# Attention outputs stored in two steps for pairs 1 to 14, and two projection steps per unit of attention at its end

## The chip, the cores and the metric

The kernel runs on one core of one Trainium2 chip. The metric is device time in microseconds (us) of one execution. All executions quoted here are fast: only those are compared. "Before" is the kernel before the change; it was run again in the same rounds as every other kernel, on the same chip.

## The reference, cut to what matters

The program has two independent parts; their outputs stand side by side. Part A is a state-space layer, which this text doesn't touch. Part B is attention over 64 segments of 32 tokens with 8 memory tokens each, 32 heads of 128, and an output projection:

```python
for s in range(n_seg):                       # 64 segments
    h = jnp.concatenate([mem, xs], axis=1)   # 8 memory rows, 32 new rows
    q, k, v = h @ Wq, h @ Wk, h @ Wv         # 32 heads of 128
    p = softmax(where(mask, q @ k.T * scale, -1e9))
    o = einsum('bhte,hed->btd', p @ v, Wo)   # output projection, 4096 -> 1024
    mem = o[:, :M, :]
    outs.append(o[:, M:, :])
```

The kernel guesses the memory rows, computes all segments at once, and checks the guess at the end. If it does not hold, a general path under a branch does the work again.

## The kernel before

The kernel issues in phases: part A's first stage with the values of part B, part A's second stage, attention, output projection. Attention goes by pairs of heads (`hp`, 16 pairs) and units (`u`, 11 a pair). The projections to queries and keys (`pr`) run ahead of it, so that TensorE (PE) has work while other engines compute exponentials. When they are used up, in the last units of the last pair, steps of the output projection (`first`) take their place. Cuts are marked with `...`.

```python
    def att_front(self, hp, u):              # scores, exponential, mask
        ...                                  # 4 matmuls on PE into s
        k.S.activation(e[:], s[0:GW, :, :, 0:GW], ACT.Exp, scale=float(E) ** -0.5, accum_out=...)
        m = self.mt[i % len(self.mt)]
        k.G.tensor_tensor(m[...], e[:], mask[...], ALU.mult)        # GpSimd (POOL)
        return [(hp, 4 * u + b, m, b) for b in range(4)]

    def att_back(self, blocks):              # values: 3 matmuls on PE from m, divided on VectorE
        ...
        early = hp == HP - 1

        def rows(g0, g1):
            r = on[64 + GX * (g0 - 1):64 + GX * (g1 - 1), :].rearrange("(g p) n -> p g n", p=GX)
            k.SP.dma_start(r[:, :, cs], ov[0:GX, g0:g1, :])
        if early and b0 + n == 2 * GE:       # half way: store what there is
            rows(1, GE)
            k.SP.dma_start(on[0:64, cs], ov[0:64, 0, :])
        if b0 + n == 2 * NG:                 # the pair is done
            if early:
                rows(GE, NG - 1)
            else:
                rows(1, NG - 1)
                k.SP.dma_start(on[0:64, cs], ov[0:64, 0, :])
            ...

    def attention(self):
        for hp in range(HP):
            for u in range(NU):
                ...
                pend += self.att_front(hp, u)
                back(8)                      # values lag two units (8 blocks) behind
                yield hp, u
        back(0)                              # the final flush
        yield HP, 0

    def outproj_first(self):                 # a step is four 128x512 matmuls
        ...
        for tt in range(3):
            ps.append(k.ps("P"))
            for h in range(0, 24, 4):        # 18 steps need heads 0 to 23 only
                self.out_mm(ps[tt], self.ol0, tt, 0, h, h + 4)
                yield
        ...                                  # from here on heads 24 to 31, b_ol

        for n, (hp, u) in enumerate(at):     # in kernel_main
            ...
            if done == 18 * HP:              # query/key projection used up
                if first is None:
                    ...
                    first = b.outproj_first()
                next(first)
        p3.close()
        ...
        f0 = nc.values_load(b.flag[0:1, 0:1], min_val=0, max_val=1)
        with tc.If(f0 == 1, preferred_fallthrough_block=True, label="general"):
            ...                              # the general path: not taken here
```

`SP` is the engine that issues most DMAs, in order. In attention a scheduler may reorder the matmuls of PE, so the program's text alone doesn't give the order; it was read from the built program.

## Time and profile before

| | before |
|---|---|
| time | 1247.49 us median of 3 runs (1247.3 to 1248.05) |
| PE busy | 1234.4 of 1245.6 us |
| waits of PE from 480 to 1030 us | 0.9 us, all on POOL's b_m |
| last copy of output to the end of the span | 4.4 us |

The first lines are from the page of before: the span; busy time of PE, its share and its instructions; and the chain of work that ended last, by engine.

```profile
span 1245.6 us, 20120 instructions
...
PE 1234.4 (99%) x8270; PEld 662.3 (53%) x8342; DVE 668.0 (54%) x1250; ACT 263.5 (21%) x631; POOL 275.8 (22%) x407
...
PE 98%; DMA 1%; issue 0%; ACT 0%; POOL 0%; DVE 0%; SPq 0%; ACTq 0%
```

This is the list of waits of PE in before, from 480 to 1030 us: who waited for whom, us in total, times, longest.

```profile
PE psO L64 <- POOL b_m L644: 0.9, 3, 0.4
```

The timeline of PE in before shows the three. Its columns are start, duration, engine, line, operation, output and inputs, shapes, number of matmuls merged, and in brackets the idle time before and what ended it. psS are scores, psO and psR values, psP with b_wv, b_vst or b_ol the output projection.

```profile
1008.39 0.34 PE L64 MATMUL psS<-b_q,b_k 128*128 128x99 bf16 x4
1008.57 0.28 PE L64 MATMUL psO<-b_v,b_m 128*128 128x129 bf16 x2
1009.05 0.23 PE L64 MATMUL psO<-b_v,b_m 128*128 128x129 bf16 x1 [0.20 <-POOL b_m L644]
1009.11 1.03 PE L64 MATMUL psP<-t,b_wv 128*128 128x512 bf16 x4
...
1011.53 0.22 PE L64 MATMUL psO<-b_v,b_m 128*128 128x129 bf16 x1
1012.01 0.29 PE L64 MATMUL psO<-b_v,b_m 128*128 128x129 bf16 x2 [0.26 <-POOL b_m L644]
1012.13 1.03 PE L64 MATMUL psP<-t,b_vst 128*128 128x512 bf16 x3
...
1015.42 0.39 PE L64 MATMUL psO<-b_v,b_m 128*128 128x129 bf16 x4
1016.24 0.29 PE L64 MATMUL psO<-b_v,b_m 128*128 128x129 bf16 x2 [0.43 <-POOL b_m L644]
1016.37 0.28 PE L64 MATMUL psR<-b_v,b_m 128*128 128x129 bf16 x2
...
1025.98 5.13 PE L64 MATMUL psP<-t,b_ol 128*128 128x512 bf16 x23
```

The SP queue of before, with the DMAs that the argument uses. The duration is the queue's own, not the transfer's.

```profile
936.50 0.40 SPq L64 DMA_DIRECT2D b_wq<-in_B_Wq_dram  x1
940.08 0.39 SPq L64 DMA_DIRECT2D b_wk<-in_B_Wk_dram  x1
...
1006.91 9.47 SPq L64 DMA_TRANSPOSE b_ol<-b_on  x1
...
1017.68 5.92 SPq L64 DMA_DIRECT2D b_on<-b_ob  x2
...
1024.84 17.64 SPq L64 DMA_TRANSPOSE b_ol<-b_on  x4
```

### The profile page before, as it was taken

To read this page: it belongs to the slowest core of one execution; us is meant where nothing else is said; L and a number is where in the kernel's file an instruction comes from. 1 tells how busy PE (TensorE), PEld (TensorE's weight loads), DVE (VectorE), ACT (ScalarE), POOL (GpSimd) and SP (SyncE) were. 2 spreads that over 40 slices of the span, in tenths; PEclk is the share of its full clock that TensorE was granted. 3 is DMA by queue.
4 is the path that set the end of the run, shared out by engine and by line. 5 is a ranking of instruction groups with operands and counts; after the bars stand their busy time and mean duration, and the time that the engine had idled before them with its cause. 6 is when DMAs were issued, how large, how long until landed. Compare 5 with 4: busy or idle time off the path is not lost.

```text
span 1245.6 us, 20120 instructions
## 1 busy us (share of the span) xinstructions
PE 1234.4 (99%) x8270; PEld 662.3 (53%) x8342; DVE 668.0 (54%) x1250; ACT 263.5 (21%) x631; POOL 275.8 (22%) x407
## 2 busy tenths in 40 slices
PE   9999999999999999999999999999999999999998
PEld 5444444444455555556666656555665554446444
DVE  4688899998711124666666666666666641001000
ACT  5344444443310000211112111111211110000000
POOL 4111331212332321322222222222222220000000
PEclk9999999999999999999999999999999999999999
DMA  9965444554898834664454544545473289407000
GB/s 245 272 192 148 131 132 128 144 156 107 241 323 247 251 116 95 192 167 123 95 144 108 144 108 114 138 92 133 96 155 95 61 223 220 110 18 153 17 17 27
DMA packets 316022, 176.83 MB, mean 142 GB/s; under 512 B 138650, under 2 KB 301326, under 8 KB 315926
## 3 DMA queue, kind: packets, MB, share of 16 engines
q1 hardware_dynamic: 293830, 147.95, 48.1%
q10 hardware_dynamic: 21072, 24.38, 5.9%
q0 software_dynamic: 1024, 3.17, 0.7%
q8 instruction: 66, 1.08, 0.4%
q14 instruction: 30, 0.25, 0.1%
HBM read 89.14 MB, written 53.17 MB: 114 GB/s over the span
## 4 chain that ended last, share of the span: by engine, by line
PE 98%; DMA 1%; issue 0%; ACT 0%; POOL 0%; DVE 0%; SPq 0%; ACTq 0%
PE psP L64 82%; PE psU L64 9%; PE psS L64 3%; PE psO L64 2%; PE psR L64 2%; DMA wo<-in_B_Wo_dram 1%; DMA b_xr<-in_B_x_dram 0%; ACT b_xe L89 0%; POOL b_m L644 0%; DVE b_ost L91 0%; SPq L64 0%; ACT b_e L641 0%; ACTq L89 0%
## 5 line engine op out<-in xcount | busy, mean ns | idle before, releaser
L64 PE MATMUL psP<-b_xe,b_wq 128*128 128x480 bf16 (+1 forms) x1280 | 247.7, 343 | 0.1
L64 PE MATMUL psP<-b_xe,b_wk 128*128 128x480 bf16 (+1 forms) x1280 | 247.7, 343 | 0.0
L64 PE MATMUL psP<-b_wv,b_xe 128*128 128x512 bf16 (+2 forms) x1033 | 223.4, 372 | 1.0 <-ACT b_xe L89 0.2
L644 POOL TENSOR_TENSOR b_m<-b_e,maskB 99x396 bf16<-99x396 bf16 x160 | 139.8, 874 | 334.0 <-ACT b_e L641 334.0
L641 ACT ACTIVATE b_e<-psS 99x396 bf16<-99x396 f32 x176 | 88.2, 501 | 532.2 <-PE psS L64 527.9
L64 PEld LDWEIGHTS <-b_wk 128*128 128x128 bf16 x1280 | 119.4, 98 | 94.2
L64 PEld LDWEIGHTS <-b_wq 128*128 128x128 bf16 x1280 | 118.7, 98 | 87.7
L64 PEld LDWEIGHTS <-b_xe 128*128 128x128 bf16 x1056 | 101.8, 98 | 119.1 <-ACT b_xe L89 0.4
L91 DVE CAST b_k<-psP 128x480 bf16<-128x480 f32 (+1 forms) x192 | 97.5, 529 | 101.1 <-PE psP L64 101.1
L91 DVE CAST b_q<-psP 128x480 bf16<-128x480 f32 (+1 forms) x192 | 97.5, 529 | 93.0 <-PE psP L64 91.4
L64 PEld LDWEIGHTS <-b_ol 128*128 128x128 bf16 x864 | 84.3, 98 | 94.4
L64 PE MATMUL psU<-a_xT,a_bt 128*128 128x512 bf16 x493 | 113.9, 379 | 1.1
L64 PE MATMUL psP<-t,a_hl 128*128 128x512 bf16 x496 | 112.1, 379 | 0.8
L91 DVE CAST b_ost<-psP 128x512 bf16<-128x512 f32 (+1 forms) x17 | 11.5, 676 | 183.4 <-PE psP L64 182.4
L64 PE MATMUL psP<-wo,b_ol 128*128 128x512 bf16 (+1 forms) x440 | 91.9, 364 | 0.4
L64 PE MATMUL psP<-t,b_ol 128*128 128x512 bf16 x408 | 91.7, 379 | 0.4
L280 POOL TENSOR_SCALAR a_tt<-a_pr,a_tabf 128x1 f32<-128x1 f32 x48 | 34.1, 709 | 243.5 <-DVE a_pr L275 243.5
L89 ACT ACTIVATE b_vst<-psP 128x512 bf16<-128x512 f32 x126 | 72.0, 589 | 71.0 <-PE psP L64 65.0
L661 DVE TENSOR_TENSOR b_ob<-psO,b_accR 99x384 bf16<-99x384 f32 x160 | 85.9, 553 | 2.0
L267 DVE TENSOR_TENSOR a_pr<-psU,a_tabf 128x2048 f32<-128x2048 f32 x32 | 73.0, 2282 | 15.7 <-PE psU L64 14.0
L64 PEld LDWEIGHTS <-a_bt 128*128 128x128 bf16 x512 | 49.2, 98 | 57.6
L64 PEld LDWEIGHTS <-a_hl 128*128 128x128 bf16 x512 | 49.1, 98 | 56.7
(200 smaller groups left out, 963.8 us busy)
## 6 DMA issues: line engine op xcount, KB each, us to landing
b_v<-b_vx SPq DMA_DIRECT2D x16, 1122.0 KB
b_wv<-in_B_Wv_dram SPq DMA_DIRECT2D x16, 1024.0 KB
b_on<-b_ob SPq DMA_DIRECT2D x15, 960.0 KB
b_vx<-b_vst ACTq DMA_DIRECT2D x24, 544.0 KB
a_hs<-a_h SPq DMA_DIRECT2D x32, 256.0 KB
b_wog<-in_B_Wo_dram SPq DMA_DIRECT2D x4, 2048.0 KB
b_wq<-in_B_Wq_dram SPq DMA_DIRECT2D x16, 512.0 KB
b_wk<-in_B_Wk_dram SPq DMA_DIRECT2D x16, 512.0 KB
```

Source lines behind the costliest of these rows:

```text
L64: r = f(*a, **kw)
L89: self.S.activation(out, in_, ACT.Copy)
L91: self.V.tensor_copy(out, in_)
L267: V.tensor_tensor(pr[:], u[:].unsqueeze(1).to_broadcast([128, 2, 2, TB]), view(t3, [[TB + 1, 2], [TB + 1, 2], [1, TB]]), ALU.mult)
L280: G.tensor_scalar(tt[:, j:j + 1], w[:, j, TB - 1:TB], t3[:, 1, TB:TB + 1], None, ALU.mult)
L641: k.S.activation(e[:], s[0:GW, :, :, 0:GW], ACT.Exp, scale=float(E) ** -0.5, accum_out=self.accE[0:GW, i:i + 1])
L644: k.G.tensor_tensor(m[0:GW, 0:4 * GP].rearrange("p (a b q) -> p a b q", a=2, b=2)[:, :, :, 0:GW], e[:], mask[0:GW, :, :].unsqueeze(2).to_b ...
L661: V.tensor_tensor(self.ob[:, b0:b0 + n, :], o[0:GW, 0:n, 0:E], r.unsqueeze(2).to_broadcast([GW, n, E]), ALU.mult)
```

## The change

It has two parts, numbered here as in the prediction. Part 1 takes two steps of the output projection instead of one with each of the last units of attention, to give PE something to do while it would wait for the mask. Part 2 stores each pair's outputs in two portions, as only the last pair's were stored before; its intent is presumably to spread the traffic. Pair 0 is left out.

```diff
@@ att_back
-        early = hp == HP - 1
+        early = hp > 0
@@ kernel_main
                     first = b.outproj_first()
                 next(first)
+                next(first)
         p3.close()
```

In the built program part 2 adds 14 DMA issues to SP. Part 1 leaves PE the same matmuls in another order from 1006 us on.

## The prediction

> **What bounds it.** TensorE. The page gives PE 1234.4 us busy of a 1245.6 us span (99%), and the chain of waits is 98% PE. By windows of time, PE is 430.0 of 430 us busy from 560 to 990 us. From 485 to 1030 us, all of attention and the start of the output projection, PE's list of waits has only three, on POOL's masked probabilities b_m, 0.9 us together. The timeline puts them in the last units of attention: 0.20 us before 1009.05, 0.26 before 1012.01, 0.43 before 1016.24.
>
> **Part 1, two projection steps per unit.** It only moves matmuls. In before, once the query/key projection is used up (1006 us), a unit of attention comes with one step: four 128x512 matmuls, 0.86 us (32 take 6.91 us in the timeline, 216 ns each; the Trainium skill, "TensorE: Matmul & The Clock Gate", section "Back-to-back issue gap", has N / 2.4 + 2.5 ns: the trace agrees). With scores and values a unit then costs PE about 1.3 us, while scores, exponential (0.50), accumulator read (0.19) and mask (0.87), with hand-overs, take about 1.9 us until values may start. So PE catches up with POOL three times. With two steps a unit costs 2.1 us. The compiled order of the changed kernel has eight such matmuls where four stood, in each of the last units and before the final flush, so each wait gets 0.86 us more cover. I expect all 0.9 us to vanish; PE is the chain, so all of it counts.
>
> What could give it back: attention ends about 5 us later (1016 to about 1022), so its last stores, issued at 1017.7, come at about 1023. The transposed loads of row block 1 follow in the SP queue (1024.8 to 1042.5, so to about 1048); first use is 1065.7, some 15 us of slack. The transposed load b_ol of the first row block depends on early stores only (issued 1006.9); PE reaches it after the same work, at about 1025. The steps taken inside attention use heads 0 to 23, loaded long before.
>
> **Part 2, stores in two steps for pairs 1 to 14.** 14 more DMA issues on SP (about 0.3 to 0.5 us each), same bytes. In the compiled order the early store now stands ahead of the next query and key weight loads and waits for DVE's b_ob. The Trainium skill, "DMA: Bandwidth & Descriptors", section "Anatomy of one DMA", says that the issuing sequencer waits, not the DMA engines; so the weight loads behind are delayed, an estimated 0 to 4 us. Their slack is about 37 us (issued 936.5, first used 973.5). No PE wait on a DMA shows in attention, so this wins and costs nothing.
>
> **Sum.** 1247.5 - 0.9 = 1246.6 us, 0.07%; range 1245.9 to 1247.9. Chances: faster 0.004, same 0.988, slower 0.008.
>
> **What would show it.** Right: no PE wait on b_m between 1005 and 1025; PE busy unchanged at 1234 us; attention's last matmul near 1022; b_ol's first matmul near 1025 without a wait; no PE idle in attention before 1005. Wrong: a PE or weight-load wait on a DMA (b_ol, wo, b_wq, b_wk, b_v), or a b_m wait left at the flush.
>
> **What would make it wrong.** The b_ol load lands just before its use, so reaching it 0.9 us sooner exposes it; or early stores, held in the SP queue, delay a pair's value or weight loads more than estimated. Either would cost 1 to 5 us.

## The result, and the profile after

The change took 1246.90 us median (1246.65 to 1247.20, 4 runs), and before 1247.47 (1247.30 to 1248.05; the three runs above and a fourth). The ratio is 0.9995, with a 95% interval of 0.9977 to 1.0012. Ratios here are the mean time of one kernel's fast runs over that of the other's of the same rounds, so not quite the ratio of the medians. Repeated in other rounds (last experiment) it was 0.13 us below before. So a difference exists at most in the tenths, and this document asks where the rest went, because the trace shows 1.4 us of PE time saved.

The page of the change:

```profile
span 1245.3 us, 20124 instructions
...
PE 1234.2 (99%) x8270; PEld 662.5 (53%) x8342; DVE 667.7 (54%) x1250; ACT 263.4 (21%) x631; POOL 275.8 (22%) x407
...
PE 99%; issue 0%; DVE 0%
```

The list of waits of PE from 480 to 1030 us is empty. The timeline of PE, at the same places:

```profile
1010.04 0.34 PE L64 MATMUL psS<-b_q,b_k 128*128 128x99 bf16 x4
1010.22 0.33 PE L64 MATMUL psO<-b_v,b_m 128*128 128x129 bf16 x3
1010.39 1.89 PE L64 MATMUL psP<-t,b_vst 128*128 128x512 bf16 x8
...
1020.58 0.50 PE L64 MATMUL psO<-b_v,b_m 128*128 128x129 bf16 x6
1020.92 0.28 PE L64 MATMUL psR<-b_v,b_m 128*128 128x129 bf16 x2
...
1024.49 5.13 PE L64 MATMUL psP<-t,b_ol 128*128 128x512 bf16 x23
```

The groups of three value matmuls take 0.17 us now (1010.22 to 1010.39), the six of the flush 0.34 (1020.58 to 1020.92) where before took 0.95 (1015.42 to 1016.37). The three savings are 0.37, 0.43 and 0.61 us, together 1.41. From the start of the last matmul on b_wk to that of the first on b_ol it is 20.03 us in before and 18.62 in the change: 1.42. From there to the last matmul both take 214.52 us.

The SP queue of the change:

```profile
937.79 1.31 SPq L64 DMA_DIRECT2D b_on<-b_ob  x2
939.21 0.53 SPq L64 DMA_DIRECT2D b_wq<-in_B_Wq_dram  x1
940.01 0.39 SPq L64 DMA_DIRECT2D b_wk<-in_B_Wk_dram  x1
...
1022.24 2.66 SPq L64 DMA_DIRECT2D b_on<-b_ob  x2
...
1026.41 17.62 SPq L64 DMA_TRANSPOSE b_ol<-b_on  x4
```

The query weights are issued 2.7 us later, behind the new early store, and nobody waits for them: the last matmul on b_wk starts at 1005.87 us, in before at 1005.95. Up to the end of the work the prediction holds, but for the size of what part 1 wins. Now the end. These are the last copy of the output on VectorE (DVE), and what SP waited for longest in its last lines: first before, then the change.

```profile
1240.81 0.42 DVE L91 CAST b_ost<-psP 128x256 bf16<-128x256 f32 x1 [6.24 <-PE psP L64]
...
SPq L1155 <- SPq L1155: 1.3, 2, 0.8
```

```profile
1239.32 0.42 DVE L91 CAST b_ost<-psP 128x256 bf16<-128x256 f32 x1 [6.24 <-PE psP L64]
...
SPq L1156 <- SPq L1156: 2.8, 1, 2.8
```

The work ends 1.49 us earlier, but the span only 0.35 us. The stretch from the end of that copy to the end of the span is 4.38 us in before and 5.51 in the change (unrounded records): 1.13 us were given back. And SP waits for itself, once, for 2.8 us. The records of SP's sequencer (the part of an engine that takes its instructions in order) around its last branch, with times from the end of the copy. DRAIN is the name of an instruction that stands a few times at its end:

```
                                     before    change
last output store issued              +0.03     +0.03
its data landed                       +1.21     +1.21
its semaphore complete                +1.70     +1.75
SP's last branch                      +0.41     +0.40
two instruction fetches, 8 KiB each   +1.51     +1.59
next instruction of SP                +0.95     +3.26
SP's first DRAIN                      +3.36     +4.61
end of the span                       +4.38     +5.51
```

The next instruction of SP checks a semaphore. In the change that semaphore belongs to a store issued at 1170.84 us, whose completion came at 1172.97. So SP did not wait for data. The records don't tell which engine the fetches are for. SP is the last engine to get to the common end: the other engines' last DRAIN before it starts at +0.90 at the latest, SP's at +3.55 in before and +4.69 in the change.

SP goes on 2.31 us later, and yet only 1.13 reach the end. In before SP goes on early, but its second check is for the last store: it passes at +1.72, when that store's semaphore is complete, 0.75 us after the first check; in the change, where the store is long done, the second check follows after 0.08. That is 0.67 us. And before loses about 0.44 us at the first DRAIN, which starts 0.36 us after the check in front of it and takes 0.13 (in the change 0.04 and 0.01).

### The profile page after: what moved, and what is told of

The parts are those of the page before. It is cut to its first block, busy times and chain, and to the rows that moved or that the text cites. A ratio compares the mean times of both kernels' runs of the same rounds, so it can differ in the third digit from the quotient of the medians.

```text
span 1245.3 us, 20124 instructions
## 1 busy us (share of the span) xinstructions
PE 1234.2 (99%) x8270; PEld 662.5 (53%) x8342; DVE 667.7 (54%) x1250; ACT 263.4 (21%) x631; POOL 275.8 (22%) x407
## 4 chain that ended last, share of the span: by engine, by line
PE 99%; issue 0%; DVE 0%
PE psP L64 82%; PE psU L64 9%; PE psS L64 3%; PE psO L64 2%; PE psR L64 2%; DVE b_xe L91 0%; DVE b_ost L91 0%; DVE a_n L962 0%; DVE hpb L105 0%; DVE ones L102 0%
```

## The experiments

The theory: part 2 of the prediction's count is wrong. The 14 added issues move the code of SP, which decides how long SP takes from its last branch to the end; part 1 alone is worth 1.4 us. Rivals: the end is longer because the work ends earlier, or by chance; the order of completions decides; or the split stores cost something themselves. For part 1 a rival says that the order of the projection matmuls, not the mask, is what counts.

In the table, "SP" is the number of SP's instructions in front of the final branches in the built program. "PE part" is the time from the start of the last b_wk matmul to that of the last matmul. "Stretch" runs from the end of the last copy to the end of the span. Time and difference are medians, in us; before is that of the same rounds.

| kernel | time | before | difference | SP | PE part | stretch |
|---|---|---|---|---|---|---|
| before | 1247.47 | | | 569 | 234.55 | 4.38 |
| change | 1246.90 | 1247.47 | -0.57 | 583 | 233.14 | 5.51 |
| e1_two_steps | 1246.04 | 1247.54 | -1.50 | 569 | 233.14 | 4.42 |
| e2_split_stores | 1248.56 | 1247.54 | +1.02 | 583 | 234.56 | 5.42 |
| e3_change_sp_hint | 1246.82 | 1247.54 | -0.72 | 584 | 233.13 | 5.41 |
| e4_two_steps_sp_hint | 1246.10 | 1247.54 | -1.44 | 570 | 233.13 | 4.39 |
| e5_before_pad16 | 1248.62 | 1247.32 | +1.30 | 586 | 234.56 | 5.39 |
| e6_before_pad8 | 1248.18 | 1247.32 | +0.86 | 578 | 234.56 | 5.52 |
| e7_change_moved14 | 1245.70 | 1247.32 | -1.62 | 569 | 233.13 | 4.34 |
| e8_zero_steps | 1247.03 | 1247.32 | -0.29 | 569 | 234.40 | 4.39 |
| e9_mask_on_vector | 1246.11 | 1247.07 | -0.96 | 569 | 233.26 | 4.35 |
| e10_three_steps | 1245.86 | 1247.07 | -1.21 | 568 | 233.13 | 4.46 |
| e11_two_steps_moved14 | 1245.09 | 1247.07 | -1.98 | 555 | 233.14 | 3.63 |
| e12_change_again | 1246.94 | 1247.07 | -0.13 | 583 | 233.13 | 5.49 |

All outputs were correct. All differences are within 0.2% of the time; the 95% intervals of the ratios contain 1 in every case but e11's (0.9970 to 0.9998). The case therefore rests on the two columns at the right more than on the timed differences. Each of their values is from one profiled execution; over all kernels of a kind they repeat within 0.01 us (PE part) and 0.13 us (stretch).

### Part 1 alone: e1_two_steps

```diff
+                next(first)
```

> Part 1 alone (two steps per unit, stores as in before). Both theories: no PE wait on b_m from 1005 to 1025 us, first b_ol matmul about 1.4 us earlier than in before (1025.98), last DVE copy of b_ost near 1239.3 us. Theory (the stretch from the end of that copy to the end of the span, 4.4 us in before and 5.6 in the change, grows because of the 14 added DMA issues on SP, which move SP's code): stretch 4.4 us, span near 1244.1, about 1.3 us faster than before, so about 1245.9 to 1246.2 on the clock. Rival (the stretch is longer because the work ends earlier, or varies by chance): stretch 5.0 to 5.6 us, no faster than the whole change (1246.9).

Measured: 1246.04 us (1245.75 to 1246.29) against 1247.54 (1247.17 to 1248.30): 1.50 us less, in ranges that don't meet. The PE part is that of the change, the stretch that of before. The last copy came at 1239.74, 0.4 us later than expected, because of another wait: PE waited 0.4 us at 492 us, labelled "issue", before the first value matmul of all. Such a wait of 0.2 to 0.4 us stands in the profiles of e3, e4 and e6 as well, and not in those of before or the change. It is not explained here; it is the reason that the stretches of a run are compared and not its absolute times. The rival that an earlier end makes a longer stretch falls: the work ends 1.1 us earlier than in before, and the stretch is 4.42.

### Part 2 alone: e2_split_stores

```diff
-        early = hp == HP - 1
+        early = hp > 0
```

> Part 2 alone (stores in two steps, one projection step per unit). Theory: PE as in before, three waits on b_m, 0.9 us as listed; last DVE copy near 1240.8 us; stretch after it 5.4 to 5.7 us instead of 4.4; 0.8 to 1.2 us slower than before, about 1248.4. Rival (stretch not tied to SP's issues): stretch 4.4 us, time as before, 1247.5.

Measured: 1.02 us slower (1247.95 to 1248.91, which overlaps before's 1247.17 to 1248.30), PE as in before with its three waits, stretch 5.42. The end of e2:

```profile
1240.73 0.42 DVE L91 CAST b_ost<-psP 128x256 bf16<-128x256 f32 x1 [6.24 <-PE psP L64]
...
SPq L1155 <- SPq L1155: 2.7, 1, 2.7
```

The copy ends when it does in before, and SP again has one wait for itself, 2.7 us. So the whole loss is part 2's, and behind the work. The two parts add up: -1.50 + 1.02 = -0.48, and the change measured -0.57.

### A branch hint for SP: e3_change_sp_hint and e4_two_steps_sp_hint

The kernel gives PE a hint about its final branch some 25 us ahead. If SP waits for the instructions at the branch's target, the same hint on SP might help.

```diff
-    k.tc.mark_branch_hint_location("general", "LikelyTaken", engines=[mybir.EngineType.PE])
+    for e in (mybir.EngineType.PE, mybir.EngineType.SP):
+        k.tc.mark_branch_hint_location("general", "LikelyTaken", engines=[e])
```

> The whole change, and in addition a branch prefetch hint on SP, beside the one that PE has, some 25 us before the branch at the end. Theory (SP waits for the instructions at the branch's target): SP goes on within 1 us after its last branch, stretch 4.4 us or less, about 1245.7 to 1246.2. Rival (SP's stretch is about DMA completion or chance): unchanged, stretch 5.6, 1246.9.

> Part 1 alone with the SP hint. Theory: the branch's target is at hand without a hint, so equal to part 1 alone within 0.3 us (stretch 4.4). Rival: a hint shortens the stretch in any kernel, so it is over 0.5 us faster than part 1 alone.

The hint was executed (SP has it at 1213.04 us in e3), and it did nothing clear of the scatter: stretch 5.41 with it on the change, 4.39 with it on part 1. For e3 the theory's number missed. Either the wait is not for the branch's target, or the hint has no effect on SP in this place; these runs don't tell which.

### Useless instructions: e5_before_pad16 and e6_before_pad8

These leave attention and its stores as they are and only add SP instructions early, at about 200 us.

```diff
+        pad = k.drp.tile([16, 128], BF16, name="b_pad")
+        for i in range(16):
+            k.SP.dma_start(pad[i:i + 1, :], z[0:1, 0:128])
```

> The kernel before with 16 tiny, useless stores (256 bytes each) put on SP near 200 us, where SP has slack. Sixteen, because the last stores of a kernel take turns on eight semaphores: the last store keeps its semaphore while SP's code behind it moves by 16 instructions or a few more. Theory (position of SP's code): PE as in before, stretch from the last DVE copy to the end 5.4 to 5.5 us instead of 4.4, and 1.0 us slower (1248.5). Rival (which semaphore the last store uses decides, so that the eight waits at the end come in a lucky order): stretch 4.4, 1247.5.

> The same with 8 stores. If a block boundary of the instructions decides, the stretch is a step: either 4.4 or 5.4 to 5.5 us, nothing between. If every added issue costs something, about 4.9 us.

Measured: stretches of 5.39 (e5) and 5.52 us (e6), PE part as in before. SP's waits for itself in its last lines, first e5, then e6:

```profile
SPq L1158 <- SPq L1158: 2.4, 1, 2.4
```

```profile
SPq L1158 <- SPq L1158: 2.8, 1, 2.8
```

So it need not be the stores of attention; stores that write 4 KB to an unused place, a thousand microseconds earlier, do the same. The rival about the last store's semaphore falls, for this 1.0 us, with e5: the last store has number 102 in before, e5 and e6 alike. Eight and sixteen (9 and 17 more instructions in the built program) cost the same, so it is a step and not a price per issue. In e5 the time rose by 0.3 us more than the stretch explains; in e6 by 0.3 us less. The spread of the runs is of that size.

### The change with SP's count put back: e7_change_moved14

```diff
+            q = k.G if hb < 7 else k.SP
-            k.SP.dma_start(self.vx[hb][64 + NMX:GX, :], z[0:GX - 64 - NMX, :])
-            k.SP.dma_start(self.vx[hb][T + 32:NSLOT, :], z[0:32, :])
+            q.dma_start(self.vx[hb][64 + NMX:GX, :], z[0:GX - 64 - NMX, :])
+            q.dma_start(self.vx[hb][T + 32:NSLOT, :], z[0:32, :])
```

> The whole change, with 14 of the zero-fill stores of 200 us moved from SP's queue to GpSimd's, so that SP has as many instructions as in before. Theory: stretch back at 4.4 us with the split stores still in place, as fast as part 1 alone (1246.0). Rival (the split stores themselves, or their traffic, cost the 1.0 us): stretch 5.4, 1246.9.

Measured: 1245.70 us, 1.62 less than before, with stretch 4.34 and all split stores in place. The end of e7:

```profile
1239.26 0.42 DVE L91 CAST b_ost<-psP 128x256 bf16<-128x256 f32 x1 [6.24 <-PE psP L64]
...
SPq L1157 <- SPq L1157: 1.2, 2, 0.7
```

SP's single wait for itself of 2.8 us is gone. This settles it from the other side: the split stores themselves cost nothing; what they add to SP's count does. Count here is of instructions or of DMA issues: the edit moves both.

### No explicit step: e8_zero_steps

```diff
-                next(first)
+                if False:
+                    next(first)
```

> The kernel before with no projection step per unit (the scheduler may still put some matmuls there). Theory of part 1 (PE catches up with POOL): several more waits on b_m in the last units, at 0.3 to 0.8 us each, 2 to 4 us later than before at the first b_ol matmul, 1249.5 to 1251.5. Rival (the 1.4 us of part 1 come from something else in the moved matmuls): no more waits on b_m, time within 0.5 us of before.

Measured: both missed. There is one wait on b_m, and the kernel is no slower than before (-0.29 us). The timeline of PE in e8 tells why:

```profile
1006.84 0.34 PE L64 MATMUL psS<-b_q,b_k 128*128 128x99 bf16 x4
1007.79 0.23 PE L64 MATMUL psO<-b_v,b_m 128*128 128x129 bf16 x1 [0.62 <-POOL b_m L644]
1007.86 0.38 PE L64 MATMUL psP<-t,b_wv 128*128 128x512 bf16 x1
...
1010.35 0.81 PE L64 MATMUL psP<-t,b_wv 128*128 128x512 bf16 x3
```

With the step taken from the loop, the scheduler, which is free here, moved the later projection matmuls (b_wv) between the units on its own, one to three at a time. The edit did not make the dose zero, so the run does not test what it was made for. It shows that the text's order is not PE's order in this phase.

### The mask on another engine: e9_mask_on_vector

```diff
-        k.G.tensor_tensor(m[0:GW, 0:4 * GP]...
+        q = k.V if hp == HP - 1 and u > 3 else k.G
+        q.tensor_tensor(m[0:GW, 0:4 * GP]...
```

> The kernel before (one step per unit, stores as in before), with the mask multiplication of the last pair's units 4 to 10 on VectorE instead of GpSimd. This takes away what the waits are for, with the order of the matmuls kept up to the final flush. Theory (PE catches up with a mask that takes 0.87 us on POOL): if VectorE's mask takes under 0.5 us, two or three of the three waits go and the last matmul on b_wk to the first on b_ol takes 18.6 to 19.2 us instead of 20.03, at one step per unit; about 1246.3 to 1246.9. Rival (the 1.4 us lie in how the projection matmuls are spread, not in the mask): 19.9 to 20.1 us, 1247.4.

This is the test of part 1 that e8 was not: before's one step per unit, but a faster mask. The groups of instructions in e9, from 995 to 1020 us, have

```profile
L645 DVE TENSOR_TENSOR b_m<-b_e,maskB 99x396 bf16<-99x396 bf16 x7 | 2.6, 365 | 0.6 <-ACT b_e L641 0.5
```

365 ns a mask, where POOL took 873 ns in the same window of before:

```profile
L644 POOL TENSOR_TENSOR b_m<-b_e,maskB 99x396 bf16<-99x396 bf16 x10 | 8.7, 873 | 14.3 <-ACT b_e L641 14.3
```

The waits on b_m are gone from the list, and the last b_wk matmul to the first on b_ol takes 18.74 us instead of 20.03: 1.29 of the 1.42 us, at one step per unit. The time, 1246.11 us, is 0.2 us below the range that was expected. The rival falls: what part 1 covers is the mask's latency on POOL.

### Three steps: e10_three_steps

```diff
-                next(first)
+                for _ in range(3):
+                    next(first)
```

> Three steps per unit, stores as in before. Theory: two steps leave no wait, so a third has nothing to win: no wait on b_m, the stretch of PE from the last b_wk matmul to the end as long as with two steps (within 0.1 us), 1246.0. If the transposed load b_ol, now needed about 1.5 us sooner, lands just before its use, as the prediction feared, a PE wait on b_ol appears and it is slower than two steps by up to 2 us.

Measured: PE part 233.13 us, as with two. Two steps leave nothing. b_ol, used at 1024.29 us, was not waited for.

### The fastest version: e11_two_steps_moved14

Part 1 with the edit of e7: stores as in before, and 14 zero-fills moved from SP to GpSimd.

> Two steps per unit, stores as in before, and 14 zero-fill stores moved from SP to GpSimd, so that SP has 14 instructions fewer than in before: the candidate for the fastest version. Theory (a step at a block boundary): stretch 4.4 us or, if a second, shorter stall at SP's drain moves out of the way too, 3.9 to 4.3 us; 1245.5 to 1246.0. Rival (every SP instruction costs about 0.07 us at the end): stretch 3.4 us, 1245.0.

Measured: 1245.09 us, 1.98 less than before and the fastest of all, in ranges that don't meet (1244.90 to 1245.34 against 1246.84 to 1247.40). The end of e11:

```profile
1239.20 0.42 DVE L91 CAST b_ost<-psP 128x256 bf16<-128x256 f32 x1 [6.24 <-PE psP L64]
...
SPq L1157 <- SPq L1157: 1.0, 2, 0.5
```

The stretch is 3.63 us, another 0.79 less than in e1, and below the 3.9 that the theory named as its best; the time, too, is below the theory's range and nearer to the rival's 1245.0. There is a second step, at SP's DRAIN: in e1 it starts 0.50 us after the check in front of it and takes 0.14 us; in e11, 0.04 and 0.01. That is 0.59 of the 0.79 us. The other 0.19 goes with the order of the checks, which end at +2.70 us instead of +2.89: the last store's semaphore is checked fourth in e11 and second in e1, so fewer checks are left when it is complete (+1.63 and +1.60). The rival, a price of 0.07 us per instruction, expected 3.4, and from this run alone the two can hardly be told apart; but e5 and e6 refute it, with 5.39 us at 16 more stores and 5.52 at 8 more.

### The change again: e12_change_again

> The whole change again, beside the others. Both theories: stretch 5.4 to 5.6 us, 0.5 to 0.7 us faster than before, 0.9 to 1.1 us slower than part 1 alone.

Measured: stretch 5.49 us, PE part 233.13, time 0.13 us below before instead of 0.57. The profile repeats to two hundredths, the timed difference to some tenths. Its expectation of 0.5 to 0.7 us was missed for that reason.

## Why the prediction was right or wrong

- **Total, right, for reasons that were partly wrong.** It said 1246.6 us in 1245.9 to 1247.9, and 1246.90 was measured. Two errors, 0.5 us too little won and 1.0 us of cost left out, went against each other. In part that was luck, and the range was wide enough to hold before's own 1247.5.
- **Part 1's mechanism, right.** "So PE catches up with POOL three times": the three waits are gone (list of waits, timeline), and e9 removes them by a faster mask as well.
- **Part 1's size, off.** "I expect all 0.9 us to vanish" was mis-sized: 1.42 us vanished. The sum of the idle times was taken for the time lost. The profile counts idle time from the end of the matmul before, and that end is modelled. The Trainium skill, "Perfetto Trace Analysis", section "Summary: the profiler window per engine type", says that for TensorE the reported end is an estimate. This trace agrees: value matmuls are shown 0.22 to 0.23 us long and start 0.057 us apart (0.17 us for three) when none waits. So each wait hides some 0.16 us of lost time (0.22 less 0.057), three of them 0.5, an estimate from those two numbers. 0.9 + 0.5 is 1.4.
- **What part 1 might give back, right.** Attention's last matmul starts at 1020.98 us (said: about 1022), last stores at 1022.24 us (said: about 1023), transposed loads done in the queue at 1044.03 (said: about 1048), first b_ol matmul at 1024.49 (said: about 1025), no wait on b_ol.
- **Part 2 within attention, right.** The weight loads' issue moved by 2.7 us (estimate: 0 to 4) and PE did not wait. The Trainium skill, "DMA: Bandwidth & Descriptors", section "Anatomy of one DMA", says that it is the issuing sequencer which waits for a semaphore, and not the DMA engines. The section describes DMAs that GpSimd issues, though its sentence on waiting is not limited to them; for SP this trace agrees: b_wq, issued at 936.50 in before, stood behind the store until 939.21.
- **Part 2 as a whole, wrong.** The step that failed is "so this wins and costs nothing", in the sense that it has no price. It looked for costs only where PE might wait. The 14 issues lengthened SP's way from its last branch to the end by 1.0 us (e2; stretch 5.42 against 4.38), and nothing runs beside that.
- **What stays open.** That what is added to or taken from SP decides, in steps (555 instructions: stretch 3.63, of which 0.19 less for the order of the checks; 568 to 570: 4.34 to 4.46; 578 to 586: 5.39 to 5.52), is shown. Whether the steps go by SP's instructions or by its DMA issues is not: but for the one hint of e3 and e4, all that was added or moved were DMA issues. The same count of other instructions on SP would tell. The cause of the steps is argued, not shown. The Trainium skill, "Runtime: NRT & Kernel Launch", section "Instruction fetch mechanics", says that instructions are fetched in blocks ahead of use, and that a taken branch whose target is not at hand makes the sequencer wait for a fetch. A target that slips over a block's boundary would give such a step, and SP's wait with nothing outstanding fits. The fetches are no evidence: the records don't say for whom they are, and the same pair stands in before (+1.51) and e11 (+1.50), where SP has gone on at +0.95 and +0.94, before they start. And the hint of e3 changed nothing.

## What to carry to other kernels

Read what a wait costs from start to start of the instructions around it, against a group that does not wait; the idle time that is listed may leave a good part out. When a change has two parts, run each alone: here one won 1.5 us and the other lost 1.0, and together they looked like almost nothing. Agreement of a predicted total says little when two errors of opposite sign can hide in it. If added instructions stand on the engine that finishes the program, compare the stretch from the last useful work to the end of the span; when it has jumped, a few instructions more or fewer on that engine, or on another engine instead, are a cheap thing to try.

## What the Trainium skill lacked or had wrong

- "Runtime: NRT & Kernel Launch", "Instruction fetch mechanics", warns of the stall behind a branch and gives no size for it. If that is what it is, SP lost 2.3 us between its branch and its next instruction here (0.54 us in before, 2.86 in the change), of which 1.0 to 1.1 us reached the end of the program; the rest was time that SP otherwise spends on the last store's completion and at its DRAIN. No page says that adding instructions far ahead of the branch can bring it on: 8 tiny stores at about 200 us did (e6).
- The same section speaks of blocks of 16 KiB. The trace has two instruction queues: on one a fetch is 16 KiB, on the other 8 KiB, in pairs at the end. Whom each serves is not recorded.
- No page of the skill covers branch hints. On PE this kernel has one; on SP it had no effect (stretch 5.41 with it, 5.51 and 5.49 without).
- "TensorE: Matmul & The Clock Gate", "Back-to-back issue gap", gives about 131 ns a matmul for sustained streams of weight loads and matmuls of 512 columns, and calls N / 2.4 + 2.5 ns too much there. This kernel's stream of exactly that kind runs at 216 ns (32 in 6.91 us), which is what the formula says. The prediction cites the formula without the page's reservation.
- No page says that idle time in front of a matmul is understated by the modelled end; the numbers above are 0.9 us listed and 1.42 us lost.
